# Rank-32 mixer kernel: h of groups 0 and 1 from three row tiles of TensorE, and the V slice for it loaded onto 96 partitions by one transfer

## The chip, the cores and the metric

The kernel runs on 1 core of one Trainium2 chip. The metric is device microseconds (us) of one execution. The kernel before has a median of 325.66 us over 3 runs (325.48, 325.66 and 458.61 us).

The engines are named as the profile names them: PE is TensorE's matmul, PEld its weight load, DVE is VectorE, ACT is ScalarE, POOL is GpSimd, SP is SyncE. POOL issues the software transfers (queue q0 of the profile), SP the hardware ones (q1).

## What is computed

The reference has two stages. A short causal filter along the sequence, whose 7 weights are a softmax and differ between 8 groups of 24 channels; and then a mixer, whose first half is a rank-32 product along the sequence and whose second half is a two-layer product along the channels. With x of 8 x 4224 x 192:

```python
w = softmax(weight)                          # 8 x 7
y[b,s] = sum_k w[h,k] * x_pad[b, s+k]        # conv, per head of 24 channels
h = (y.T @ U) @ V                            # U 4224 x 32, V 32 x 4224
u = y + h.T
out = u + relu(u @ w_ch1) @ w_ch2            # 192 -> 768 -> 192
```

## The kernel before

**Tiles and groups.** The sequence of each batch is cut into 33 row tiles of 128 positions; 8 batches make 264 row tiles, in 33 groups of 8 (GT = 8). A group's work is: u of its 8 tiles, the transposed u (`uT`, 128 partitions: two halves `hf` of 64 channels, times three chunks `c` of 64 channels), W1 with Relu (`w1`, line 554, Relu on ACT at line 568 and on DVE at line 570), W2 (`w2`, line 583) with the final addition on DVE (line 592) and the store from SP's queue (line 600).

**The rank-32 product.** For each batch, `tt_mm` (line 402) sums y.T @ U over the tiles, and the result is copied to SBUF as bf16 (`tt_sb`, line 422): 128 partitions which hold four copies of the same 32 rows (the matrix R4 of lines 741 and 428 sums four partial results and repeats the sum). `h_tiles` (line 457) multiplies slices of V (`V_sb`) by `tt_sb` for later groups, in four row tiles of 32 partitions each, and DVE adds y to it (line 479). SP's transposing transfer (line 498) then makes `uT`.

**Groups 0 and 1 of batch 0.** These two groups do not take that path: their transposed u is made on PE alone. `yT_part` (line 509) multiplies y by the identity into PSUM, and `hT_part` (line 524) accumulates h on top of it, with `ttb[0]` (that is `tt_sb`) as the stationary operand and `V0_sb`, the first 2048 columns of V, as the moving one; ACT and DVE then copy PSUM to `uT` (lines 256 and 258, in `evac`). In `hT_part` the contraction is over 32 partitions, and each matmul of chunk c uses partitions 0 to 31 of both operands, whatever c is; its two halves `hf` go to the output columns 0 to 63 and 64 to 127 of the array. The list `parts` says which chunk and which of the four tile indices `i` share a PSUM bank: group 0 has five parts (chunk 0 in two, chunk 1 in one, chunk 2 in two), so 10 matmuls of 256 or 512 columns; group 1 has three parts, so 6 matmuls of 512 columns.

**Order of the work.** The schedule is written out by hand (`manual_schedule`): each engine runs its instructions in program order. Lines 690 to 752 are the prologue. On PE: filter of batch 0 (line 369), U layout (line 264), `tt_mm`, the last partial sum (lines 741 and 682), and then `hT_part(0)`, `yT_part(1, rest)`, `hT_part(1)` (lines 749 to 752). After that the loop over SLOTS begins with `w1(0)`, then h of group 2 (`do("h2")`, the first use of `V_sb`), then `w1(1)` and `w2(0)`.

**The software queue.** POOL issues, in this order: two x loads of batch 0 (line 79), two U loads (lines 123 and 127), two more x loads, the V0 load (line 133), four W1 loads (line 137), one x load of batch 1, four `V_sb` loads (line 715), a fifth (line 722), the W2 load (line 726), three x loads of batch 1. All of them read float32 in DRAM and write bf16 to SBUF. Eight semaphores serve POOL's transfers in turn, so that an issue waits until the eighth transfer before it has landed. The profile leaves buffer numbers out, so that it shows V0_sb as V_sb, and W1_sb as W_sb.

The V0 load before is one transfer of 32 rows: 8,192 bytes of float32 are read for each row, and 4,096 bytes of bf16 written. A W1 load has 64 partitions outermost and the three chunks in the middle:

```python
out=W1_sb[HB * hf : HB * hf + HB, :, m0:m1],
in_=moe_w_ch1[:, m0:m1].rearrange("(c k) m -> k c m", k=HB),
```

Of the kernel before, what the change touches and what calls it, by code (L numbers as in the profile page):

```python
# [9 lines left out]
BF16 = mybir.dt.bfloat16  # L10
# [4 lines left out]
def kernel(  # L15
# [10 lines left out]
    nc = tc.nc  # L26
    P = nc.NUM_PARTITIONS
# [3 lines left out]
    R = moe_U.shape[1]  # L31
# [4 lines left out]
    GT = 8  # L36
# [3 lines left out]
    HB = P // 2  # L40
# [4 lines left out]
    cst = ctx.enter_context(tc.tile_pool(name="cst", bufs=1))  # L45
# [57 lines left out]
    def iota(t, pattern, base, mul):  # L103
# [20 lines left out]
        out=Ur[:, 0:nfull, :], in_=U4[0 : nfull * P, :].rearrange("(k p) c -> p k c", p=P)  # L124
# [4 lines left out]
        x_piece(k)  # L129


    V0_sb = cst.tile([R, 2 * GT * P], BF16, name="V0_sb")
    nc.gpsimd.dma_start(out=V0_sb[:], in_=moe_V[:, 0 : 2 * GT * P])
    W1_sb = cst.tile([P, 3, M4], BF16, name="W1_sb")
    for m0, m1 in ((0, 2 * P), (2 * P, M4)):
        for hf in range(2):
            nc.gpsimd.dma_start(
                out=W1_sb[HB * hf : HB * hf + HB, :, m0:m1],
                in_=moe_w_ch1[:, m0:m1].rearrange("(c k) m -> k c m", k=HB),
# [27 lines left out]
    for hh in range(2):  # L167
# [3 lines left out]
        out=dif[:], in0=dif[:], scalar1=rq[:, 0:1], scalar2=None, op0=ALU.add  # L171
# [5 lines left out]
        out=d_sb[:],  # L177
# [8 lines left out]
        out=hot[:],  # L186
# [6 lines left out]
        out=ident[:], in0=fp[:], scalar1=float(P), scalar2=None, op0=ALU.is_equal  # L193
# [9 lines left out]
        out=c_sb[:].rearrange("p k h -> p h k"),  # L203
# [5 lines left out]
    for hh in range(2):  # L209
# [3 lines left out]
            out=pr[:],  # L213
# [8 lines left out]
        out=Eq[:], in0=efp[:], scalar1=rq[:, 1:2], scalar2=None, op0=ALU.is_equal  # L222
# [3 lines left out]
        out=fp[:], in0=fp[:], scalar1=R - 1, scalar2=None, op0=ALU.bitwise_and  # L226
# [3 lines left out]
        out=R4[:], in0=fp[:], scalar1=0.0, scalar2=None, op0=ALU.is_equal  # L230
# [23 lines left out]
    def evac(eng, out, in_):  # L254
        if eng == "A":
            nc.scalar.activation(out=out, in_=in_, func=ACT.Copy)  # L256
        else:
            nc.vector.tensor_copy(out=out, in_=in_)  # L258
# [135 lines left out]
    ttb = [[] for _ in range(B)]  # L394
# [123 lines left out]
    def hT_part(g, parts):  # L518

        uTt[g] = uts.tile([P, 4, 3, P], BF16, name="uT")  # L520
        for c, i0, i1, p, _ in parts:
            for hf in range(2):
                t0 = (2 * g + hf) * 4 * P
                nc.tensor.matmul(  # L524
                    out=p[HB * hf : HB * hf + HB, 0 : (i1 - i0) * P],
                    lhsT=ttb[0][0:R, HB * c : HB * c + HB],
                    rhs=V0_sb[:, t0 + i0 * P : t0 + i1 * P],
                    start=False,
                    stop=True,
                    tile_position=(0, HB * hf),  # L530
                )
        for c, i0, i1, p, eng in parts:
            evac(
                eng,
                uTt[g][:, i0:i1, c, :],
                p[:, 0 : (i1 - i0) * P].rearrange("p (i t) -> p i t", t=P),
            )
# [161 lines left out]
    for r, (k0, k1) in KP[2].items():  # L699
        j = NB0 // 2 * r + k0  # L700
        nc.gpsimd.tensor_copy(
            out=U4_sb[:, o : o + k1 - k0, :, :],
            in_=U_sb[:]
# [9 lines left out]
    for q in range(4):  # L713
        src = moe_V[:, 0 : full * 8 * P].rearrange("r (k q t) -> r k q t", q=4, t=2 * P)
        nc.gpsimd.dma_start(
            out=V_sb[32 * q : 32 * q + 32, 0 : 2 * full, :].rearrange(
                "r (k a) t -> r k (a t)", a=2
            ),
            in_=src[:, :, q, :],
# [3 lines left out]
        out=V_sb[0:32, 2 * (NT // 8), :], in_=moe_V[:, (NT - 1) * P : NT * P]  # L723
# [23 lines left out]
    yT_part(1, parts1)  # L747
    tt_done(0, ps0)
    hT_part(0, parts0 + more)
    rest = [(c, 0, 4, bank(), "ADA"[c]) for c in (1, 2)]  # L750
    yT_part(1, rest)
    hT_part(1, parts1 + rest)
    band2 = cst.tile([P, H, QB], BF16, name="band2")
    for xp in XP[1:]:
        x_part(1, *xp)
    for r in range(4):
        q = slice(QB * r, QB * r + QB)
        for hh in range(2):
            nc.gpsimd.tensor_copy(
                out=band2[q, HQ * hh : HQ * hh + HQ, :],  # L760
                in_=bands[hh][q, :, HB * (r % 2) : HB * (r % 2) + QB],
# [86 lines left out]
```

## Time and profile before

| what | value |
|---|---|
| median of 3 runs | 325.66 us |
| span of the profiled execution, first to last instruction | 323.2 us |
| median less that span | 2.46 us |
| PE busy | 317.6 us, 98% of the span |
| DVE, ACT, POOL busy | 268.6, 170.0, 142.7 us |
| software queue q0 | 38,192 packets, 14.73 MB |
| hT_part matmuls (line 524) | 16, from 18.3 to 20.1 us |
| first W1 matmul (line 554) | 20.45 us |
| first matmul that uses V_sb (line 457) | 24.44 us |

A whole execution's own time is not listed for the profiled run; its span and what lies around it are taken together as the median. The views used are: the page's busy shares and its rows of forty slices; the chain of work that ended last, followed back from the end, where each piece is shown with its start, its length, the engine and the line; the timeline of one engine (start, length, what, how many, and in brackets the idle time before it and who ended it); and the rows of one source line, with the least, median and greatest duration in ns and, for a transfer, the time from issue to landing. The trace also has one record for each packet of a transfer (start, duration, size) and one for each of the sixteen times that a transfer's landing is counted.

### The profile page before, as it was taken

The numbers are of one execution on the slowest core, as the hardware profiler recorded it, in microseconds if no ns is written. First come the engines' busy times: TensorE is split into PE (matmuls) and PEld (weight loads), VectorE is DVE, ScalarE is ACT, GpSimd is POOL, SyncE is SP. The second block draws the span as 40 slices with busy tenths as digits, with TensorE's granted clock in tenths as the row PEclk, the third lists the DMA queues.
The fourth block names the chain that finished last, engine by engine and source line by source line (L and its number), as shares of the span: only waits on it lengthen the run. The fifth ranks groups of instructions, "written<-read, shape, count | busy, mean of one in ns | idle before, by whom it ended". The sixth has DMA issues, their size and how long they took to land.

```text
span 323.2 us, 9583 instructions
## 1 busy us (share of the span) xinstructions
PE 317.6 (98%) x3996; PEld 223.7 (69%) x3996; DVE 268.6 (83%) x551; ACT 170.0 (53%) x344; POOL 142.7 (44%) x111
## 2 busy tenths in 40 slices
PE   8999999999999999999999999999999999999995
PEld 3747676478677647866864884687797497487495
DVE  6769989987977986997898699789888897896863
ACT  1766724860874397088239609824903902912910
POOL 8764179728957983992897497000000000000000
PEclk9999999999999999999999999999999999999999
DMA  9999993999998999599499957138268059048035
GB/s 106 192 191 183 206 209 100 196 192 257 208 135 200 246 142 190 166 189 209 130 237 192 181 149 194 52 105 231 61 178 262 3 150 275 18 121 271 2 121 173
DMA packets 122906, 53.51 MB, mean 166 GB/s; under 512 B 87760, under 2 KB 122832, under 8 KB 122864
## 3 DMA queue, kind: packets, MB, share of 16 engines
q1 hardware_dynamic: 84528, 38.08, 45.4%
q0 software_dynamic: 38192, 14.73, 39.2%
q8 instruction: 31, 0.51, 0.7%
q10 hardware_dynamic: 144, 0.10, 0.1%
q14 instruction: 11, 0.09, 0.1%
HBM read 29.49 MB, written 25.95 MB: 172 GB/s over the span
## 4 chain that ended last, share of the span: by engine, by line
PE 92%; ACT 3%; DMA 2%; DVE 1%; issue 0%; POOL 0%; POOLq 0%
PE ps L583 42%; PE ps L554 39%; PE ps L339 3%; PE ps L457 3%; DMA x_sb<-in_x_dram 2%; PE ps L402 2%; ACT rl_sb L568 2%; PE ps L369 1%; ACT y_sb L256 1%; PE ps L509 1%; DVE u_sb L479 1%; DVE rl_sb L570 1%; PE ps L524 0%; PE ps L428 0%; POOL x_sb L79 0%
## 5 line engine op out<-in xcount | busy, mean ns | idle before, releaser
L568 ACT ACTIVATE rl_sb<-ps 128x512 bf16<-128x512 f32 x233 | 124.3, 604 | 108.0 <-PE ps L554 96.0
L583 PE MATMUL ps<-W_sb,rl_sb 128*128 128x192 bf16 x1584 | 141.2, 246 | 0.2
L583 PEld LDWEIGHTS <-rl_sb 128*128 128x128 bf16 x1584 | 128.3, 98 | 11.8 <-issue 11.5
L554 PE MATMUL ps<-uT,W_sb 64*128 64x512 bf16 x1188 | 131.7, 376 | 0.0
L570 DVE TENSOR_SCALAR rl_sb<-ps 128x512 bf16<-128x512 f32 x163 | 105.3, 688 | 15.7 <-PE ps L554 15.4
L554 PEld LDWEIGHTS <-W_sb 64*128 64x128 bf16 x1188 | 66.9, 94 | 60.4 <-issue 3.9
L592 DVE TENSOR_TENSOR out_sb<-ps,u_sb 128x384 f32<-128x384 f32 (+1 forms) x133 | 70.4, 551 | 25.5 <-PE ps L583 25.0
L305 POOL COPY xb_sb<-x_sb 32x3072 bf16<-32x3072 bf16 (+1 forms) x24 | 67.4, 2824 | 0.5
L479 DVE TENSOR_TENSOR u_sb<-y_sb,ps 128x192 bf16<-128x192 bf16 (+1 forms) x168 | 66.3, 461 | 0.0
L293 POOL COPY xb_sb<-x_sb 128x3072 bf16<-128x3072 bf16 x12 | 32.7, 2742 | 42.1 <-PE ps L339 32.2
L256 ACT ACTIVATE y_sb<-ps 128x384 bf16<-128x384 f32 (+4 forms) x90 | 38.3, 520 | 9.7 <-PE ps L339 7.4
L79 POOL DMA_DIRECT2D x_sb<-in_x_dram x32 | 27.0, 848 | 9.6 <-PE ps L457 3.8
L258 DVE CAST y_sb<-ps 128x408 bf16<-128x408 f32 (+4 forms) x36 | 19.1, 578 | 1.3 <-PE ps L369 1.0
L457 PE MATMUL ps<-tt_sb,V_sb 32*128 32x192 bf16 x264 | 12.4, 246 | 0.1
L339 PE MATMUL ps<-x_sb,band 64*32 64x384 bf16 x192 | 12.1, 333 | 0.0
L339 PE MATMUL ps<-xb_sb,band 64*32 64x384 bf16 x192 | 12.1, 332 | 0.0
L457 PEld LDWEIGHTS <-V_sb 32*128 32x128 bf16 x264 | 4.7, 92 | 7.3 <-issue 7.3
L416 ACT ACTIVATE tt_hi<-ps 128x192 bf16<-128x192 f32 x8 | 2.6, 330 | 11.9 <-PE ps L402 11.9
L369 PE MATMUL ps<-x_sb,band 64*64 64x240 bf16 (+3 forms) x192 | 8.0, 276 | 0.2 <-DMA x_sb<-in_x_dram 0.2
L339 PEld LDWEIGHTS <-band 64*32 64x32 bf16 x384 | 4.5, 89 | 5.2 <-issue 2.4
L153 PE MATMUL ps<-zz 128*128 128x512 f32 (+1 forms) x10 | 6.7, 816 | 1.1 <-DVE zz L143 1.1
L369 PEld LDWEIGHTS <-band 64*64 64x64 bf16 x192 | 6.0, 106 | 2.1 <-issue 1.4
(65 smaller groups left out, 71.3 us busy)
## 6 DMA issues: line engine op xcount, KB each, us to landing
out_dram<-out_sb SPq DMA_DIRECT2D x131, 192.0 KB, 2.7
x_sb<-in_x_dram POOLq DMA_DIRECT2D x14, 384.0 KB, 6.9
x_sb<-in_x_dram POOLq DMA_DIRECT2D x7, 432.0 KB, 6.7
x_sb<-in_x_dram POOLq DMA_DIRECT2D x7, 408.0 KB, 8.0
x_sb<-in_x_dram POOLq DMA_DIRECT2D x1, 504.0 KB, 7.3
uT<-u_sb SPq DMA_TRANSPOSE x31, 3.5
x_sb<-in_x_dram POOLq DMA_DIRECT2D x1, 480.0 KB, 5.6
W_sb<-in_moe_w_ch_dram POOLq DMA_DIRECT2D x2, 192.0 KB, 7.8
```

Source lines behind the costliest of these rows:

```text
L79: return nc.gpsimd.dma_start(out=xt[b][HB * r : HB * r + HB, s0:s1, :], in_=x[b, blk * HB : (blk + s1 - s0) * HB, :].rearrange("(j p) d -> ...
L256: nc.scalar.activation(out=out, in_=in_, func=ACT.Copy)
L293: nc.gpsimd.tensor_copy(out=xbt[b][:, s0:s1, :], in_=xt[b][:, s0 + 1 : s1 + 1, :])
L305: nc.gpsimd.tensor_copy(out=xbt[b][q, s0:s1, :], in_=xt[b][q, s0:s1, :])
L339: nc.tensor.matmul(out=pp[r][QB * cg : QB * cg + QB, 0 : nk[r] * GS], lhsT=w[hr], rhs=t[hr, st : st + 2 * nk[r] - 1 : 2, hs], start=True, ...
L457: nc.tensor.matmul(out=banks[pr][:, a * D : (a + 1) * D], lhsT=V_sb[32 * q : 32 * q + 32, (j // 8) * 2 + j % 2, :], rhs=ttb[b][32 * q : 32 ...
L479: nc.vector.tensor_tensor(out=u_group(g)[:, i : i + n, :, hf, :], in0=yt[b][:, run[0] : run[0] + n, :].rearrange("p n (c k) -> p n c k", c=3),
L554: last = nc.tensor.matmul(out=pps[m][hf][:], lhsT=W1_sb[HB * hf : HB * hf + HB, c, m * P : (m + 1) * P], rhs=uTt[g][HB * hf : HB * hf + HB ...
L568: nc.scalar.activation(out=rl[:, m, hf, :], in_=pp[hf][:], func=ACT.Relu)
L570: nc.vector.tensor_scalar_max(out=rl[:, m, hf, :], in0=pp[hf][:], scalar1=0.0)
L583: last = nc.tensor.matmul(out=cps[:, a * D : (a + 1) * D], lhsT=rlt[g][:, m, hf, (i + a) * P : (i + a + 1) * P], rhs=W2_sb[:, m, :], start ...
L592: nc.vector.tensor_tensor(out=o[:, 0:n, :].rearrange("p n (c k) -> p n c k", c=3), in0=cps[:, 0 : n * D].rearrange("p (n c k) -> p n c k", ...
```

## The change

`V0_sb` becomes 96 partitions high, and holds the same 32 rows of V three times. One transfer of the software queue fills it: its source has a new outermost dimension of step 0 and count 3. In `hT_part`, chunk c takes both operands from the partitions 32c to 32c + 31, and its tile position in the array moves to row 32c, so that the three chunks use three row tiles. The order of instructions on each engine is left as it was, and so is their number.

```diff
@@ -129,8 +129,11 @@
-    V0_sb = cst.tile([R, 2 * GT * P], BF16, name="V0_sb")
-    nc.gpsimd.dma_start(out=V0_sb[:], in_=moe_V[:, 0 : 2 * GT * P])
+    V0_sb = cst.tile([3 * R, 2 * GT * P], BF16, name="V0_sb")
+    v0 = moe_V[:, 0 : 2 * GT * P]
+    nc.gpsimd.dma_start(
+        out=V0_sb[:], in_=bass.AP(v0.tensor, v0.offset, [[0, 3]] + [list(d) for d in v0.ap])
+    )
@@ -523,11 +526,11 @@
                 nc.tensor.matmul(
                     out=p[HB * hf : HB * hf + HB, 0 : (i1 - i0) * P],
-                    lhsT=ttb[0][0:R, HB * c : HB * c + HB],
-                    rhs=V0_sb[:, t0 + i0 * P : t0 + i1 * P],
+                    lhsT=ttb[0][R * c : R * c + R, HB * c : HB * c + HB],
+                    rhs=V0_sb[R * c : R * c + R, t0 + i0 * P : t0 + i1 * P],
                     start=False,
                     stop=True,
-                    tile_position=(0, HB * hf),
+                    tile_position=(R * c, HB * hf),
                 )
```

## The prediction

> **What bounds the kernel now.** I read the page first: shares, the row of the clock, the chain.
>
> ```profile
> PE 317.6 (98%) x3996; PEld 223.7 (69%) x3996; DVE 268.6 (83%) x551; ACT 170.0 (53%) x344; POOL 142.7 (44%) x111
> ...
> PEclk9999999999999999999999999999999999999999
> ...
> PE 92%; ACT 3%; DMA 2%; DVE 1%; issue 0%; POOL 0%; POOLq 0%
> ```
>
> PE is busy from end to end, and 92% of the chain is PE's. What stops PE early is not won back: there is no slack behind it. Next, the chain of waits around the edit.
>
> ```profile
> 18.35 0.83 PE ps L524 x10
> 19.18 0.57 PE ps L509 x16
> 19.75 0.76 PE ps L524 x6
> 20.51 1.23 PE ps L554 x10
> 21.74 3.04 ACT rl_sb L568 x6
> 24.79 0.04 issue
> 24.83 4.16 PE ps L554 x36
> 28.99 0.28 PE ps L457 x8
> ```
>
> All 16 edited matmuls lie on the path, 0.83 + 0.76 us, and the W1 matmuls follow at once. Then the V0 load: the rows of its line, and POOL's timeline behind it.
>
> ```profile
> L133 POOL DMA_DIRECT2D V_sb<-in_moe_V_dram x1: 564/564/564, 7.2 to 7.2; - x1
> ...
> DMA to landing us min/median/max: 7.9/7.9/7.9
> ```
>
> ```profile
> 7.75 1.28 POOL L137 DMA_DIRECT2D W_sb<-in_moe_w_ch_dram x2
> 9.88 0.62 POOL L137 DMA_DIRECT2D W_sb<-in_moe_w_ch_dram x1 [0.84 <-DMA x_sb<-in_x_dram]
> 11.38 0.63 POOL L137 DMA_DIRECT2D W_sb<-in_moe_w_ch_dram x1 [0.88 <-DMA Ur<-in_moe_U_dram]
> ...
> 14.04 2.43 POOL L715 DMA_DIRECT2D V_sb<-in_moe_V_dram x4
> 17.75 0.51 POOL L722 DMA_DIRECT2D V_sb<-in_moe_V_dram x1 [1.27 <-DMA W_sb<-in_moe_w_ch_dram]
> ```
>
> V0 is issued at 7.2 and lands at 15.1; it is used at 18.35, so it has 3.2 us to spare. The waits in brackets are the rule of eight in flight. Most of the 7.9 us is queueing: landings follow one another at packet pace (V0's sixteen counts at 14.63 to 15.11, the first W1 load's to 15.62, the last W1 load's to 18.92, the four V_sb loads' to 22.40). So what is put into this queue delays all behind it. Last, PE's timeline at the start.
>
> ```profile
> 1.07 5.15 PE L153 MATMUL ps<-zz 128*128 128x512 f32 x6 [1.07 <-DVE zz L143]
> ```
>
> The trace's records of this line start 0.85 us apart up to 5.50, and 0.43 apart from 6.06: PE ran at half its clock until 5.76 us, 4.7 us after its first matmul, where the clock record begins to grant 1.0. The record falls to 0.5 at 323.2, 3.4 us after the last matmul ended (319.79).
>
> **The change part by part.**
>
> *Matmuls.* Before, the two halves `hf` of a part run side by side and the parts one after another. Group 0 has five steps of 256, 256, 512, 256 and 256 columns: 1,536 columns in 0.83 us, 0.54 ns each. After, the chunks have row tiles of their own. The second part of chunk 0 still follows the first in its row tile, and chunk 1, behind it in PE's order, starts beside it: 256 + 512 = 768 columns. The eight matmuls of line 457 show four row tiles side by side: 384 columns deep in 0.28 us, 0.73 ns each with filling and draining. At 0.73, group 0 takes 0.56 (saving 0.27) and group 1, 512 columns deep, 0.37 (saving 0.39). Sum 0.7. Bounds: nothing, if they don't overlap, and 0.9 at 0.54 ns. The copies to uT on ACT and DVE (0.47 and 0.60 us each) hide behind the 0.57 us of line 509 as now, and W1 begins with chunk 0, copied first; if that cover fails, one copy, 0.5 us, comes onto the path. I take −0.7: line 457 is the nearest row.
>
> *The issue on POOL.* One instruction as before; 0.56 us for 32 rows, 0.62 to 0.67 for a W1 load of 192 packets, so at most +0.1, off the path.
>
> *The transfer.* 96 rows in place of 32. The trace has 32 packets of 4,096 bytes, each 322 to 324 ns long. Over sixteen engines that is two each, and the landings agree: V0's follow the previous load's by 0.62 (first count) to 0.65 us (last), 0.30 to 0.31 us for each packet. The rows of before leave open how a source is dealt out whose outermost count is 3. Bounds: sixteen engines, 6 packets each, 4 more, +1.2 us; three engines, 32 each, 30 more by 0.304, +9.1 us. Rows nearest the first: the W1 loads, with a 3 in the middle but 64 outermost, landed 0.5 us apart, the pace of all sixteen (192 packets/16 = 12, by some 41 ns). Against it: no load before has its repeat outermost, and all have 32, 64 or 128 there. If queues are dealt by the outermost count, as the partitions are here, 3 gives three engines. I take three, at 0.85, since only the outermost count is new, and keep both ends.
>
> The Trainium skill speaks against this change here: DMA: Bandwidth & Descriptors, section "Rules for kernel authors", says that a leading zero-stride broadcast of c copies confines the whole transfer to at most c engines, and asks for a multiple of 16 outermost. By that rule the sum is the three-engine one below; by the W1 rows read alone it would be 325.0. No run yet shows a leading count under 16.
>
> *With three engines.* V0 lands at 15.11 + 9.1 = 24.2. POOL's other work isn't needed by PE before that. PE stands at the first matmul of line 524 from 18.35 to 24.25: +5.9. Queued behind it on PE is everything: line 509, W1, all groups; ACT and DVE wait for the uT banks. Net of the 0.7 saved, +5.2.
>
> What is late next: the loads behind V0 in the three engines, each by 9.1. W1's last lands at 28.0 in place of 18.92; the matmuls that need it (the third of six column blocks) came at about 21.74 and come at 26.9 or later: covered to within 1.1. V_sb's four loads, at 21.02 to 22.40 over the engines, become 30.1 to 31.5; PE used them at 24.44. That is a floor of +5.7 to +7.1 under the shift of all that follows, not a term to add. The rule of eight: the third V_sb issue waits for V0 and moves from about 15.2 to 24.3, the fourth waits for the first W1 load; both still stand in the queue before the engines reach them. W2 lands by 24.36 + 9.1 = 33.5 (x loads before it included), used at 29.27 + 7 = 36: covered. Batch 1's last x load, 30.92 + 9.1 = 40.0, meets the filter of 37.75 + 7 = 45: covered. The band copies on POOL (22.96) are used by line 339, slots later. SP's first transposing transfer of line 498 comes at 27.14 and shifts with its group.
>
> *The clock.* A PE that idles 5.9 us may lose its clock, as the end of the trace shows after 3.4 us. From the first edited matmul to the first Relu PE has 768 + 1,024 + 512 + 6 x 512 = 5,376 columns to do; at the pace of the W1 row (18 pairs of 512 columns in 4.16 us, 2.2 per ns) 2.4 us, and at half the clock twice that. Bounds: 0 (the clock holds), +2.4 (half all through; the 4.7 us of the start allow about as much). After that stretch the path is ACT's Relus for 3 us, which don't slow. I take +2.0, since the clock may return a little sooner.
>
> TensorE: Matmul & The Clock Gate, Part 1, says that the clock halves after a wholly idle window of about 3.4 us, with windows that run free of the program. Taken alone, as an estimate, 5.9 us of idleness holds such a window in (5.9 − 3.4)/3.4, some 7 of 10 phases; the end of this trace agrees with the 3.4. With the rule's drop the sum is +7.2, without it +5.2 or the floor.
>
> *Sum.* +5.9 − 0.7 + 2.0 = +7.2, above the floor. The profiled execution's span is 323.2, the median 325.66, so 2.46 lie around it; span after 330.4, time 332.9.
>
> **The rivals.**
>
> *A (forecast).* Three engines, clock halves: 332.9.
>
> *B. Three engines, clock holds.* The shift is the V_sb floor, +5.7 to +7.1, middle 6.4: 332.1, within 2% in somewhat more than half. For it: the drop at the end of the trace is a single row, and 5.9 exceeds 3.4 by less than a second such stretch.
>
> *C. Sixteen engines (the other side: not slower).* V0 lands at 15.11 + 1.2 = 16.3, before 18.35; W1 at 20.1, before its use at 21; V_sb at 23.6, its use moves to 23.7. Saving 0.7: 325.0. It decides as soon as V0 lands before 18.35, which is 3.2/0.304 = 10 more packets for each engine: any dealing over eight engines or more (12 packets each). Against it: the leading 3.
>
> *D. The row tiles don't overlap.* The change then doesn't do what it says on PE: 0.7 is lost in any case, 333.6 with A, 325.7 with C. Against: line 457 overlaps.
>
> *E. Longer lag.* Fewer engines than three, or the lag reaches batch 1's x loads: one engine would take 96 packets, 94 x 0.304 = +28.6. Above 336.
>
> **How the numbers follow.** Three engines 0.85, sixteen or nearly 0.13, fewer 0.02. Within three engines the clock halves in about 0.68: the idle time is 1.7 times what the trace's end needed. So A 0.58, B 0.27, C 0.13, E 0.02; D is inside each. About 2% (6.5 us; 332.2) is what a measurement of this kernel can tell from no change. A lies above it in 0.82 (its own range 331.9 to 334.6), B in 0.45, C never: 0.48 + 0.12 + 0.02, rounded to 0.61. Within 2%: 0.38; faster by 2%: 0.01, since the 1.6 us of the edited matmuls are under 6.5. The range 331.0 to 334.8 holds A and B with their ends (B's low end 325.66 + 5.7 less spread, A's high end with D and the full 2.4 and some lag) and leaves out C, E and tails, 0.2.
>
> **What would show it.** V0's issue-to-landing of 17 us (7.9 before); PE idle before line 524 of 5 to 6 us, ended by a transfer; W1 and V_sb landings 9 us later; a clock row with a dip near 24 us and slower W1 matmuls just behind it; line 524's pieces 0.5 and 0.4 us long at full clock; and from 50 us on the same profile, shifted. Wrong would be: V0 landing by 17 us (C), no dip (B), or PE waiting at line 457, W1's third block or line 583 for longer than a microsecond (a floor that I set too low).

## The result, and the profile after

The changed kernel takes 334.24 us in the median of 6 runs (333.27 to 336.18), the kernel before 325.57: a ratio of 1.0273, 95% interval 1.0244 to 1.0302, or 8.7 us more. The ratios leave out runs that took over 1.5% longer than the fastest of their kernel: one of the kernel before (458.61 us), and three of one kernel below. The profiled execution took 334.84 us with a span of 333.1.

From the page of the changed kernel: busy shares, the granted clock in forty slices, and the shares of the chain that ended last.

```profile
PE 318.8 (96%) x3996; PEld 222.4 (67%) x3996; DVE 268.7 (81%) x551; ACT 170.1 (51%) x344; POOL 143.1 (43%) x111
...
PEclk9987999999999999999999999999999999999999
...
PE 80%; DMA 12%; DVE 4%; POOL 2%; issue 1%; POOLq 0%; DVEq 0%
```

PE's busy time is almost unchanged (318.8 against 317.6 us), so the new time is waiting. 12% of the chain is now transfers (2% before), and the clock has a dip in the third and fourth slices, 17 to 33 us. The lines of the edited matmuls and of W1 are 527 and 557 here, 512 is the identity, and the V0 load is line 134. Its rows:

```profile
L134 POOL DMA_DIRECT2D V_sb<-in_moe_V_dram x1: 739/739/739, 7.2 to 7.2; - x1
...
  POOL V_sb L718: 9.8, 1
  PE ps L527: 6.1, 1
...
DMA to landing us min/median/max: 18.3/18.3/18.3
```

It takes 18.3 us from issue to landing instead of 7.9. Two instructions wait for it: PE's first edited matmul, 6.1 us, and on POOL the third V_sb load, 9.8 us, by the rule of eight in flight. The chain of the same kernel shows what the first of these waits does:

```profile
7.23 18.27 DMA V_sb<-in_moe_V_dram
25.50 0.04 issue
25.54 0.65 PE ps L527 x6
26.19 0.99 PE ps L512 x15
27.18 0.57 PE ps L527 x3
27.75 3.42 PE ps L557 x24
```

The edited matmuls are shorter (0.65 and 0.57 us, 0.83 and 0.76 before), while the identity matmuls between them, which were not touched, take 0.99 instead of 0.57: PE runs slower. The same stretch, with PEclk the granted clock (the third number from the end of a row); the last row is the first stretch in the kernel before:

```profile
22.00:25.00 3.00, 0.00 (x0) 0.00 (x0) 0.00 (x0) 0.00 (x0) 0.00 (x0) 0.55 0.23 38
25.00:27.00 2.00, 1.46 (x26) 1.01 (x25) 0.79 (x2) 0.96 (x3) 1.22 (x3) 0.50 0.24 36
27.00:29.00 2.00, 2.00 (x18) 0.63 (x16) 0.92 (x2) 1.08 (x2) 1.50 (x3) 0.50 0.77 93
29.00:31.00 2.00, 2.00 (x22) 0.91 (x20) 1.29 (x2) 1.35 (x3) 0.75 (x2) 0.97 0.92 90
...
22.00:25.00 3.00, 2.95 (x34) 1.26 (x32) 2.78 (x5) 3.00 (x7) 2.84 (x10) 1.00 1.61 190
```

The last two numbers of a row are the DMA engines' share and GB/s. The transfers run at 36 to 38 GB/s near the end of the V0 load, against 190 in the same stretch of before, and the DMA share is 0.23 against 1.61: most of the DMA engines are idle. The clock is half from 22.27 to 29.10 us. Matched by instruction, PE's two timelines give this list of how the lag grows (starts, in us):

```
                                       before   after   lag
first edited matmul                     18.34   25.54   7.20
first W1 matmul                         20.45   27.69   7.24
first use of V_sb                       24.44   32.36   7.92
W1 of group 2                           33.76   41.91   8.15
W1 of group 3                           47.12   55.68   8.56
a W2 run, about 80 us before            79.99   89.32   9.33
a W2 run, later                         92.92  102.80   9.87
the last W2 run                        307.73  317.60   9.86
```

Some three quarters of it (7.2 of 9.9 us) are there at the V0 load. In this execution PE was also 1.1 us late ahead of it (0.7 at the U layout, behind an x load; most of the rest is one wait for issue), which shortens its wait for V0 but not the lag; in the other profiled kernels with the wide load it was at most 0.4 us late there. Some 1.7 us more come after W1 of group 2, where nothing was edited. The lines on which the later part of the list rests, two from PE's timeline and one from DVE's waits between 60 and 110 us (the kernel before has none of the three):

```profile
41.91 4.06 PE L557 MATMUL ps<-uT,W_sb 64*128 64x512 bf16 x36 [0.16 <-DMA uT<-u_sb]
...
55.68 4.06 PE L557 MATMUL ps<-uT,W_sb 64*128 64x512 bf16 x36 [0.34 <-DMA uT<-u_sb]
...
DVE out_sb L595 <- DMA out_dram<-out_sb: 2.0, 1, 2.0
```

### The profile page after: what moved, and what is told of

It is laid out like the page before. It is cut to its first block, busy times and chain, and to the rows that moved or that the text cites. A ratio compares the mean times of both kernels' runs of the same rounds, so it can differ in the third digit from the quotient of the medians.

```text
span 333.1 us, 9583 instructions
## 1 busy us (share of the span) xinstructions
PE 318.8 (96%) x3996; PEld 222.4 (67%) x3996; DVE 268.7 (81%) x551; ACT 170.1 (51%) x344; POOL 143.1 (43%) x111
## 4 chain that ended last, share of the span: by engine, by line
PE 80%; DMA 12%; DVE 4%; POOL 2%; issue 1%; POOLq 0%; DVEq 0%
PE ps L557 37%; PE ps L586 35%; DMA V_sb<-in_moe_V_dram 5%; DMA uT<-u_sb 4%; PE ps L342 3%; DMA out_dram<-out_sb 3%; PE ps L460 2%; DVE u_sb L482 2%; PE ps L405 1%; DVE rl_sb L573 1%; POOL x_sb L79 1%; PE ps L372 1%; DVE out_sb L595 1%; PE ps L527 0%; PE ps L512 0%
## 5 line engine op out<-in xcount | busy, mean ns | idle before, releaser
L557 PEld LDWEIGHTS <-W_sb 64*128 64x128 bf16 x1188 | 65.3, 94 | 63.7 <-issue 5.3
L79 POOL DMA_DIRECT2D x_sb<-in_x_dram x32 | 27.1, 850 | 6.4 <-PE ps L460 2.2
L460 PE MATMUL ps<-tt_sb,V_sb 32*128 32x192 bf16 x264 | 13.1, 246 | 0.3 <-DVE u_sb L482 0.2
L261 DVE CAST uT<-ps 128x512 bf16<-128x512 f32 (+1 forms) x3 | 1.7, 600 | 7.4 <-PE ps L527 7.4
## 6 DMA issues: line engine op xcount, KB each, us to landing
V_sb<-in_moe_V_dram POOLq DMA_DIRECT2D x1, 384.0 KB, 18.3
```

Of the source, the lines that this page charges most:

```text
L79: return nc.gpsimd.dma_start(out=xt[b][HB * r : HB * r + HB, s0:s1, :], in_=x[b, blk * HB : (blk + s1 - s0) * HB, :].rearrange("(j p) d -> ...
L460: nc.tensor.matmul(out=banks[pr][:, a * D : (a + 1) * D], lhsT=V_sb[32 * q : 32 * q + 32, (j // 8) * 2 + j % 2, :], rhs=ttb[b][32 * q : 32 ...
L557: last = nc.tensor.matmul(out=pps[m][hf][:], lhsT=W1_sb[HB * hf : HB * hf + HB, c, m * P : (m + 1) * P], rhs=uTt[g][HB * hf : HB * hf + HB ...
```

## The experiments

Each ratio is against the kernel before on the same chip. Theory: the queue deals a transfer out by its outermost count, so that three DMA engines carry V0 and all that queues behind it there. Rivals: the repeated read or the tall tile is slow; the row tiles themselves cost.

**Three loads of 32 rows.**

```diff
-    nc.gpsimd.dma_start(
-        out=V0_sb[:], in_=bass.AP(v0.tensor, v0.offset, [[0, 3]] + [list(d) for d in v0.ap])
-    )
+    for c in range(3):
+        nc.gpsimd.dma_start(out=V0_sb[R * c : R * c + R, :], in_=v0)
```

> The new matmuls, but V0 comes by three software transfers of 32 rows instead of one with a repeated source. Theory (the outermost count of 3 confines the one transfer to three engines): V0's last copy lands at about 16.4 us, before its use, no wait, no dip of the clock; the row tiles save 0.7 us: 324.9 us, 0.998 of before. Rival (reading the same rows of DRAM three times, or a tile 96 partitions high, is what is slow): V0 still lands after 20 us and the time stays above 330 us. Rival (the row tiles themselves cost): no wait, but 326 us or more.

Measured: ratio 1.0048 (1.0018 to 1.0079), 326.54 us. The last V0 load has landed by 17.5 us and PE doesn't wait for it. So the same bytes, read three times into 96 partitions, are not slow. The gain on PE is there too; PE's timeline (lines 526 the edited matmuls, 511 the identity, 556 W1):

```profile
18.08 0.42 PE L526 MATMUL ps<-V_sb,tt_sb 32*64 32x256 bf16 x10
18.44 0.64 PE L511 MATMUL ps<-ident,y_sb 128*64 128x128 bf16 x16
19.00 0.41 PE L526 MATMUL ps<-V_sb,tt_sb 32*64 32x512 bf16 x6
19.35 4.06 PE L556 MATMUL ps<-uT,W_sb 64*128 64x512 bf16 x36
...
35.11 1.46 PE L556 MATMUL ps<-uT,W_sb 64*128 64x512 bf16 x6 [2.06 <-DMA uT<-u_sb]
```

From start to start the two groups of edited matmuls take 0.36 and 0.35 us, before 0.77 and 0.77: 0.8 us saved, and W1 begins 1.1 us earlier than before. But in this execution W1 of group 2 comes 1.35 us later than before, after a wait of 2.06 us for that group's transposing transfer. It was issued at 26.1 (27.1 before) and landed at 35.1 (32.3 before); batch 1's last x load, in the queue before it, landed at 34.0 (30.9 before). The theory is right on V0 (no loss there) and misses the time. The time is that of the second rival, but not for its reason: the edited matmuls are shorter, and the row tiles alone, below, cost nothing. The profiled execution is the slowest of the twelve (329.5 us); the eight with a mean clock of 0.998 or more took 325.5 to 326.9.

**The wide load with the old matmuls.**

```diff
-                    lhsT=ttb[0][R * c : R * c + R, HB * c : HB * c + HB],
-                    rhs=V0_sb[R * c : R * c + R, t0 + i0 * P : t0 + i1 * P],
+                    lhsT=ttb[0][0:R, HB * c : HB * c + HB],
+                    rhs=V0_sb[0:R, t0 + i0 * P : t0 + i1 * P],
...
-                    tile_position=(R * c, HB * hf),
+                    tile_position=(0, HB * hf),
```

> The one wide transfer of the change, but the matmuls as before: all on rows 0 to 31. Theory (the transfer makes the whole loss, and the row tiles give 0.7 us back): 0.5 to 0.9 us slower than the changed kernel, about 335.0 us. Rival (the row tiles are part of the loss): faster than the changed kernel, 333 us or less.

Measured: 1.0340 (1.0303 to 1.0378), 336.32 us. The transfer alone makes more than the whole loss, and against the changed kernel (1.0273) the row tiles give back about 2 us rather than the expected 0.5 to 0.9. In the profiled execution PE waited 6.6 us for V0, then the clock stayed at half for 7.6 us after the restart (until 32.81), against 3.6 us in the changed kernel's, and at half the clock the edited matmuls took 1.49 and 1.41 us (0.65 and 0.57 there).

**Four copies on 128 partitions.** `[[0, 3]]` becomes `[[0, 4]]`, `3 * R` becomes `4 * R`.

> The changed kernel with four copies of V0 on 128 partitions instead of three on 96: a third more bytes, outermost count 4; the fourth copy is not used. Theory (dealt by the outermost count, each engine one copy of 32 rows): V0 takes as long as in the changed kernel, landing 17.5 to 18.5 us after issue, time 334 us within 0.7. Rival (the bytes or the repeated reads set the time, whatever the engines): landing some 3.4 us later, 337 us or more. Rival (128 partitions are dealt over sixteen engines): landing at 9 to 10 us after issue, 325 to 326 us.

Measured: 1.0280 (1.0256 to 1.0303), 334.61 us, as in the changed kernel. The rows of the load:

```profile
L134 POOL DMA_DIRECT2D V_sb<-in_moe_V_dram x1: 733/733/733, 7.2 to 7.2; - x1
...
DMA to landing us min/median/max: 18.0/18.0/18.0
```

A third more bytes, and no more time. The trace's packet records say the same: in the changed kernel the 96 packets of 4,096 bytes start in three interleaved series, here the 128 in four, and within a series the starts are at first 0.305 us apart.

**A count of 3 without the repeat.** The wide load with the old matmuls, and `[[0, 3]]` replaced by `[[GT * P, 3]]`.

> The wide transfer with an outermost count of 3, but no repeat: three overlapping blocks of V, 1024 columns apart, into the 96 partitions; matmuls as before, on rows 0 to 31, which hold the right block, so that nothing of the computation changes. Theory (the outermost count deals the transfer out, repeated or not): V0 lands 17.5 to 18.5 us after issue and the time is that of the wide load with the old matmuls, 335 to 337 us. Rival (the step of 0 is what is slow): landing at 9 to 10 us after issue, time 325 to 327 us.

Measured: 1.0384 (1.0317 to 1.0452, two runs: 335.53 and 340.12 us), V0 landing after:

```profile
DMA to landing us min/median/max: 18.0/18.0/18.0
```

The repeat does not matter, the outermost count does. The time is not clearly above the wide load's with the old matmuls (the intervals overlap); in the profiled execution the clock stayed at half for 9.0 us after PE's restart at 25.28.

**The clock kept.** Six idle matmuls of zeros into a free bank, ahead of the first edited one.

```diff
+    for _ in range(6):
+        nc.tensor.matmul(
+            out=tp[:].rearrange("p (n t) -> p n t", t=P),
+            lhsT=zz[:],
+            rhs=zz[:].unsqueeze(1).to_broadcast([P, 4, P]),
+            start=True,
+            stop=True,
+        )
     hT_part(0, parts0 + more)
```

> The changed kernel with six idle matmuls of zeros, 5.1 us at full clock, just ahead of the first of the late matmuls, so that PE waits for V0 for under 1.5 us only. Theory (forecast's clock term): the granted clock stays at 1.0, and the time falls by 1 to 2.2 us against the changed kernel, to 332.0 to 333.2 us; what is left is the late V0 less the row tiles, or the late V_sb as a floor. Rival (the clock costs nothing, since ACT's Relus or the late loads bind there anyway): 334 us as in the changed kernel.

Measured: 1.0250 (1.0226 to 1.0275), 333.44 us, the clock at 1.0 throughout. The intervals of this and the changed kernel overlap, so the gain, some 0.7 us, is not clear of noise, and the time lies between the theory's 332.0 to 333.2 and the rival's 334. PE's timeline shows where a larger one went:

```profile
24.84 0.42 PE L527 MATMUL ps<-V_sb,tt_sb 32*64 32x256 bf16 x10 [0.86 <-DMA V_sb<-in_moe_V_dram]
26.11 4.46 PE L557 MATMUL ps<-uT,W_sb 64*128 64x512 bf16 x36
...
42.26 4.06 PE L557 MATMUL ps<-uT,W_sb 64*128 64x512 bf16 x36 [1.68 <-DMA uT<-u_sb]
```

W1 begins 1.6 us earlier than in the changed kernel (of these, 0.7 are V0's earlier landing), the first use of V_sb 1.85 earlier, and then PE stands 1.68 us for group 2's transposing transfer and starts W1 of group 2 at 42.26, later than the 41.91 of the changed kernel. The transfer took 8.6 us from issue, 6.8 there and 5.1 before.

**Holding an x load back.** In three kernels (the three loads, the kernel before as a control, the clock kept), batch 1's last x load was moved behind W1 of group 1, to free the way for that transposing transfer.

```diff
-    for xp in XP[1:]:
+    for xp in XP[1:3]:
...
+            if g == 1:
+                held(x_part(1, *XP[3]), ends[5])
```

> Three loads of 32 rows with the new matmuls, and the last x load of batch 1 held back until the last W1 matmul of group 1, so that it doesn't stand between group 2's u and its transposing transfer. Theory (the three loads won 1.1 us on PE by the first W1 matmul and lost 2 us at the transposing transfer, which came late behind the x loads): the wait before W1 of group 2 falls under 0.5 us, the clock holds in nearly all runs, 324.0 to 324.9 us. Rival (the transposing transfer is late for another reason): 326 us or more as without the hold.

> The kernel before with the same x load held back: the control for the row tiles. Theory (before has no wait at that transposing transfer, so nothing to win): 325.2 us within 0.4, and the three loads with the hold 0.5 to 1 us under it. Rival (the hold itself is the gain): as fast as the three loads with the hold, under 324.7 us.

> The changed kernel with the idle matmuls that keep the clock and the x load held back. Theory (with the clock kept, 1.7 us were lost again before W1 of group 2 at the late transposing transfer): that wait goes, time 331.5 to 332.5 us, which is the price of the late V0 and V_sb alone. Rival (the V_sb loads set all that follows): 333.4 us as without the hold.

Measured: three loads 1.0060 (1.0030 to 1.0090), control 1.0097 (1.0066 to 1.0127), clock kept 1.0340 (1.0293 to 1.0387); medians 328.06, 328.81 and 336.93 us. All three expectations miss in time, and the intervals of the first two overlap. In place the edit does what was wanted; PE's timeline of the three loads with the hold:

```profile
32.82 4.06 PE L556 MATMUL ps<-uT,W_sb 64*128 64x512 bf16 x36
48.62 4.06 PE L556 MATMUL ps<-uT,W_sb 64*128 64x512 bf16 x36 [2.37 <-DMA uT<-u_sb]
```

W1 of group 2 starts at 32.82 without a wait, 0.9 us earlier than before: so the wait there was indeed made by the x load (with the clock kept it goes as well, from 1.68 us to none). But the x loads of batch 2 are now the later ones (the last lands at 47.8, 45.3 before), and the next transposing transfer, group 3's, is late by 2.37 us (3.17 in the control, 1.69 with the clock kept). The wait has moved one group on, and in most runs of all three kernels the mean clock is lower as well (0.990 to 0.995). In these runs the queue has no room: what was put in, or put off, came out at a later transfer.

**The row tiles alone.** One V0 load of 32 rows and zeros in the other 64 partitions, so that the new matmuls have no transfer to pay for.

```diff
+    nc.gpsimd.dma_start(out=V0_sb[0:R, :], in_=v0)
...
     x_zero(0, nc.vector)
+    nc.vector.memzero(V0_sb[:])
```

> The row tiles alone: the new matmuls, one V0 load of 32 rows as before, and partitions 32 to 95 of V0_sb set to zero on DVE at the start, where DVE waits. It leaves out h in chunks 1 and 2 of groups 0 and 1. Theory (the row tiles save 0.9 to 1.1 us on PE by the first W1 matmul, and it is the two additional loads that take it back): that gain reaches the end, 324.0 to 324.5 us, no wait at W1 of group 2. Rival (the transposing transfer of group 2 cannot come earlier, whatever is loaded): the gain ends in a wait there, 325 us or more.

Measured: 1.0387 (1.0351 to 1.0423), 337.34 us. This is a fault of the experiment. The zeroing stands behind the load in the program and covers its rows, so it waited for the load and removed all of h from groups 0 and 1; DVE's prologue stood behind it, and PE waited for DVE:

```profile
PE ps L238 <- DVE pr L214: 12.4, 1, 12.4
```

The second try zeroes the partitions 32 to 63 on DVE and 64 to 95 on ACT, which no load writes.

> The row tiles alone, again: the run before this one zeroed all of V0_sb and so waited on DVE for the V0 load, which says nothing of the row tiles. Here only partitions 32 to 63 (DVE) and 64 to 95 (ACT) are zeroed, near the start, which waits for no load; V0 is one load of 32 rows. It leaves out h in chunks 1 and 2 of groups 0 and 1. Theory (the row tiles save 0.9 to 1.1 us on PE by the first W1 matmul, and the additional loads are what takes it back): the gain reaches the end, 324.0 to 324.5 us. Rival (the transposing transfer of group 2 cannot come earlier, whatever is loaded): the gain ends in a wait before W1 of group 2, 325 us or more.

Measured: 1.0004 (0.9988 to 1.0020), 325.75 us. W1 begins 0.8 us earlier than before, and that lead lasts without a wait until 75 us, so the rival's wait before W1 of group 2 isn't there. Four of the twelve runs end at 324.2 to 324.4 us, which is the forecast gain; the others at 325.2 to 327.3. The profiled one is the slowest of these. DVE's waits there between 60 and 110 us, of which the kernel before has the first and not the second:

```profile
DVE out_sb L599 <- PE ps L590: 5.2, 11, 1.0
DVE out_sb L599 <- DMA out_dram<-out_sb: 2.4, 1, 2.4
```

A store lands late, its buffer is not free, DVE waits, and PE waits for DVE. The changed kernel has the same wait, 2.0 us, between the 8.2 and the 9.9 of the list above; the four copies 2.6, the old matmuls with the wide load 0.9, the clock kept none. What decides in which executions the store is late stays open.

**Two loads, two row tiles.** Chunks 0 and 2 on rows 0 to 31, chunk 1 on rows 32 to 63. Against the three loads (V0_sb and the operands change likewise):

```diff
-    for c in range(3):
+    for c in range(2):
...
-                    tile_position=(R * c, HB * hf),
+                    tile_position=(c % 2 * R, HB * hf),
```

> Two loads of 32 rows instead of three, and two row tiles: chunks 0 and 2 on rows 0 to 31, chunk 1 on rows 32 to 63; nothing of the computation is left out. Half the additional bytes (the queue behind is 0.6 us later instead of 1.2) and some two thirds of the gain on PE, 0.6 us. Theory (the bytes ahead of batch 1's last x load decide when the transposing transfer lands): the wait at W1 of group 2 shrinks to under 1 us, 324.8 to 325.8 us, between before and the three loads. Rival (any additional load costs the same, by the eight in flight): 326.5 us as with three.

Measured: 0.9998 (0.9982 to 1.0014), 325.1 us, as the theory has it. W1 begins 0.6 us earlier, W1 of group 2 waits 0.22 us and that of group 3 0.32, and the lead is spent. Half the additional bytes make a tenth of the three loads' wait, in one execution of each. No kernel here beats the one before clearly.

## Why the prediction was right, and where it was off

- *Three engines.* Right, and shown: much the same landing for three copies, four copies and three blocks without a repeat (17.9 to 18.3 us from issue; 17.3 and 17.6 in the two kernels with the clock kept), 7.9 to 9.4 us in loads with 32 rows outermost, and series of packets as many as the count. The rule of the Trainium skill, "DMA: Bandwidth & Descriptors", section "Rules for kernel authors", decided well here: it speaks of any outermost dimension under 16, with the broadcast as its example, and these runs show both, with a step of 0 and with a step of 1,024 columns. The reading of the W1 loads on the other side was narrower than it was put: only the first two landed 0.5 us apart, the two larger ones 1.0 us, by their first counts. Nothing rests on it.
- *The wait for V0, +5.9.* It was too small. Measured 6.1 us, after PE had come 1.1 us late; 6.5 to 6.9 in the kernels whose PE came nearly on time; and a lag of 7.2 us at the first edited matmul. The packets' pace was right where nothing disturbed it (0.305 us for 0.304); the landing, forecast at 24.2, was 25.1 to 25.5 in the changed kernel and those three, 24.6 and 24.8 in the two with the clock kept. I had added 30 packets to V0's old landing; some packets took up to 0.69 us. Why these took longer stays open.
- *The row tiles, −0.7.* Measured 0.8 at full clock, shared out otherwise: group 0 saved 0.4 us (forecast 0.27), group 1 0.4.
- *The clock, +2.0.* It was lost, as in the likeliest case, but the term was mis-sized. With the clock kept, the time fell by 0.7 us, not by 2.0: part of what the clock costs is covered by the loads that are late in any case. The changed kernel's own runs say the same: the two with a mean clock of 0.989 took 334.7 and 334.8 us, three of the four with 0.983 to 0.985 took 333.3 to 333.8, and one 336.2.
- *The floor by V_sb, 30.1 to 31.5.* The four loads landed at 30.9 to 32.0. In the changed kernel PE came 0.3 us later than that; with the clock kept PE came earlier, and the chain runs through the last of them, landed at 31.33 us and used at 31.37.
- *What the sum left out.* I let "SP's first transposing transfer" simply shift with its group, and asked no further than 45 us. That transfer, the next one and a store were late as well: waits of 0.16 and 0.34 us on PE and 2.0 on DVE in the changed kernel; the store took 8.6 us from issue, the same store before 5.6. In the profiled execution the lag was 7.9 us at the first use of V_sb, where the sum has 7.2, and 9.9 at the end. The median is 8.7 us above before; how its runs divide is not on record.
- *The total.* 332.9 us was forecast and 334.24 measured. That they are so near is in part luck: the wait for V0 and the late transfers behind it were put too low, the clock too high.
- *The rivals.* The clock did not hold (B), all sixteen engines did not share (C), the row tiles do overlap (D). The other half of C is in doubt too: for a load over all sixteen engines I gave 325.0, and three loads over all of them took 326.5, since the edit needs 512 KB more of float32 reads from a queue that is full. A single transfer with 32 rows outermost and the repeat behind them was not run.

## What to carry to other kernels

Before a saving of PE time is counted, ask what it adds to a full transfer queue: with three loads, 1.2 us more of queue (the last W1 load landed at 20.1, 18.9 before) took back the 0.8 us of PE at a later transfer. Look at the outermost count of a software transfer: with 3 and 4 there, V0 was carried by as many DMA engines, and the loads behind it landed 9 to 10 us later too. A gain or loss that is followed only to the next wait is followed too short; compare the two timelines by instruction to the end.

## What was not expected of the hardware

The clock fell after stretches in which PE had not been idle throughout. With three loads it fell at 35.12 us, when PE had been idle for 2.06 us only, since 33.05; in the control with the held load at 49.63, after some 2.3 us of idleness. The records change on a grid of 3.41 us: all dips here last one, two, three or four such steps. With the hold on three loads PE idled 2.37 us at the same kind of place, and the clock stayed; counted on from where its clock was first granted, that idleness falls into two steps, 1.27 and 1.10 us. Counted so in all thirteen traces, the clock fell at the end of every step at full clock in which PE idled 2.06 us or more, and of none in which it idled 1.99 us or less. The spread of the three loads' runs follows it: those with a mean clock of 0.994 or 0.995 took 328.2 to 329.5 us, the others 325.5 to 326.9.

The return took longer than at the start of the kernel (4.7 us after the first matmul, before) in some executions: 3.6 us after the restart in the changed kernel, 7.6 with the old matmuls, 9.0 with the count of 3 without a repeat, although PE worked all the while. The Trainium skill, "TensorE: Matmul & The Clock Gate", Part 1, speaks of one idle window for the fall and one busy window for the return; these runs show a fall after a window that was only in part idle. The return came with the first wholly busy window in the changed kernel (25.69 to 29.10) and with the second in the other two; in those the first held edited matmuls in their old form. The other runs fit that, though no trace shows it: a dip of two steps in the trace goes with a mean clock of 0.989, three with 0.983, four with 0.979, and the ten runs of the changed kernel and the four copies lie at 0.983 to 0.989, the six with the old matmuls at 0.978 to 0.984. Whether the old form is the cause stays open.
